# Attention and MLP in one kernel: nine of sixteen key blocks in 16-bit parts

## The chip, the cores and the metric

The kernel runs on one core of a Trainium2 chip. Its metric is the time of one execution in device microseconds (us). Engines are named as in the profile: PE is TensorE (PEld its weight loads), DVE is VectorE, ACT is ScalarE, POOL is GpSimd, SP is SyncE, which here issues most transfers.

## The reference

A token's row `x` (2048 tokens of 640 numbers, all f32) is normalised. The result feeds an attention of 32 heads of 20 numbers each, and beside it an MLP of width 1536; both are added to `x`:

```python
xn = _layernorm(x)
q, k, v = split(xn @ wqkv)                       # 32 heads of 20
scores = einsum("bhqd,bhkd->bhqk", q, k) * 20 ** -0.5
p = softmax(scores)
att = einsum("bhqk,bhkd->bhqd", p, v) @ wo
mlp = gelu(layernorm(xn) @ w1 + b1) @ w2 + b2
return x + att + mlp
```

## The kernel before

**Precision.** Most products run on pairs of 16-bit numbers: a factor is written as an upper part and a remainder, and three products of parts stand for one. The product of the probabilities with V is made in one of two ways, by key block. There are 16 blocks of 128 keys, and `SPLIT` says which way a block goes.

- *Split block* (1): the upper part of the f32 exponentials is read in place as bf16 (`upper`). The remainder is made on DVE by one subtraction of 128x1024 (`rest`, L725), into a tile `low` of f16. V is kept as two f16 parts. For each of the two heads of a pair there are three products: upper by V's first part, upper by V's second part, and low by V's first part.
- *Whole block* (0): exponentials and V stay f32, with one f32 product for each head and no work on DVE. The profile counts two rows of PE for one such product.

Before, `SPLIT` is `(1, 1, 0, 0)` four times, so eight blocks are split and eight whole.

**Front (to about 226 us).** x is normalised, turned and multiplied by wqkv; Q and K go to DRAM, V stays in `vfull`, where `vproj_out` (L408, L410) writes a block in the form that `SPLIT` asks for: for a split block one copy on ACT and one subtraction on DVE, for a whole one the copy alone. POOL writes columns of ones and zeros into V beforehand (L198, L199 for a split block, L201 for a whole one).

**Attention (about 226 to 1279 us).** A unit of work is a head pair `g`, a half of the queries `hf`, a chunk `cc` of 512 queries, and a key block `kb`. `scores` (L711) makes a block's scores for both heads of the pair on PE, and ACT takes the exponential of 128x1024 of them (L713). Units run in groups of `GRP = 4` key blocks. In each group the loop emits, in this order: scores of the first two blocks; `tick()`; `rest` of the first block; a piece of filler on PE (`other`); scores of the other two blocks; `tick()`; `rest` of the remaining blocks; and `pv(prev)`, the products of the *previous* group. The four groups of one `(g, hf, cc)` add up in one PSUM tile `pv.o` of 128x512, which ACT copies out after the last (L763).

In `pv`, `product(q, ...)` (L742) writes a quarter of 32 partitions of `pv.o`, with 32 columns of V as weights. Quarters 2a and 2a+1 belong to head a, and are added later. Products with different `q` that stand next to each other run at the same time on PE. In a group of two split and two whole blocks there are, in this order: two sets of four products on the upper parts, one set of four on low (the quarter of a head is chosen by the block's place, `2 * a + n % 2`), and one set of four f32 products, again one quarter for each block and head.

**Filler.** The MLP (`layer1` L972, `layer2` L1002) and the output projection (L1085) are cut into pieces and laid between the groups by `other`, by a credit that grows by `rate = 1.265` for each place, so how much filler stands where is fixed when the program is built. Their PSUM tile (`psM`) has one buffer, which DVE reads out (L910, L938, L1043). `tick()` issues one step of each waiting piece of DVE work: GELU (L910 to L922, with tanh on ACT at L918), the additions, and the finishing of head groups (L872 to L902).

**Buffers.** `p` (exponentials) has seven, `low` has `bufs=GRP`, that is four, and the scores' PSUM tile has three. A tile takes the buffer that came free; where its last reader is a later instruction of another engine, the writer waits for that reader.

**The end.** After the attention the projection's last pieces run alone. DVE then has reduced a check of the sums to one flag. Where it is set, `general` computes the attention again in another way, in f32 and with loops; where it is not, the program ends there.

Of the kernel before, what the change touches and what calls it, by code (L numbers as in the profile page):

```python
# [9 lines left out]
F32 = mybir.dt.float32  # L10
F16 = mybir.dt.float16
BF16 = mybir.dt.bfloat16
I32 = mybir.dt.int32
AF = mybir.ActivationFunctionType
ALU = mybir.AluOpType
AX = mybir.AxisListType
PSUM = bass.MemoryType.PSUM
DRAM = bass.MemoryType.DRAM
P = 128
S, D, H, DH, F = 2048, 640, 32, 20, 1536  # L20
KD = D // P
KF = F // P
NKB = S // P
VW = DH + 1
PAD = 32 - VW
VROW = H * VW + PAD
SPLIT = (1, 1, 0, 0) * (NKB // 4)
NPAIR = H // 2
EPS = 1e-5
TOP = 15.5  # L30
# [14 lines left out]
def mha_mlp_kernel(tc, x, wqkv, wo, w1, b1, w2, b2, out):  # L45
    nc = tc.nc
    x2 = x.rearrange("b s d -> (b s) d")
    out2 = out.rearrange("b s d -> (b s) d")

    with (  # L50
# [580 lines left out]
        with ExitStack() as scope:  # L631
# [52 lines left out]
                        yield 0.7  # L684
                split_done.append(1)

            def project(ot, acc, t0, j):
                for hf in range(2):
                    cols = slice(hf * 320, (hf + 1) * 320)
                    ps = psM.tile([P, 512], F32, tag="m", name="z")  # L690
                    n = 0
                    for k in range(KD):
                        for a, b in PASS:
                            nc.tensor.matmul(ps[:, :320], ot[:, k, a, j * P : (j + 1) * P], wov[:, k, b, cols],
                                             start=(n == 0), stop=(n == 3 * KD - 1))
                            n += 1
                    nc.vector.scalar_tensor_tensor(acc[:, cols], ps[:, :320], fo, acc[:, cols], ALU.mult, ALU.add)
                nc.sync.dma_start(out2[t0 : t0 + P, :], acc)

            nfin = 2 * len(UNITS)  # L700
            checks = list(range(nfin))
# [28 lines left out]
            def pv(units):  # L730

                g, hf, cc, kb0 = units[0][:4]
                if kb0 == 0:
                    pv.o = psO.tile([P, 512], F32, tag="o", name="o")
                    pv.begun = set()
                last = units[-1][3] == NKB - 1

                def product(q, src, v0, t):
                    nc.tensor.matmul(pv.o[32 * q : 32 * q + 32, :], src[:, v0 - PAD * (1 - q % 2) :][:, :32], t,  # L742
                                     start=q not in pv.begun, stop=last, skip_group_check=True)
                    pv.begun.add(q)

                split = [(u[3], upper(u[4]), u[5]) for u in units if SPLIT[u[3]]]
                whole = [(u[3], u[4]) for u in units if not SPLIT[u[3]]]
                of16 = lambda kb, a: 2 * PAD + kb * 2 * VROW + (2 * g + a) * 2 * VW
                of32 = lambda kb, a: PAD + kb * VROW + (2 * g + a) * VW
                for kb, up, _ in split:  # L750
                    for a in range(2):
                        product(2 * a, vhalf, of16(kb, a), up[:, a])
                        product(2 * a + 1, vhalf, of16(kb, a) + VW, up[:, a])
                for a in range(2):
                    for n, (kb, _, low) in enumerate(split):
                        product(2 * a + n % 2, vhalf, of16(kb, a), low[:, a])
                for a in range(2):
                    for n, (kb, pt) in enumerate(whole):
                        product(2 * a + n % 2, vfull, of32(kb, a), pt[:, a])
                if last:  # L760
                    if cc == 0:
                        evs[g, hf] = m1.tile([P, 2, 512], F32, tag="ev", name="ev")
                    nc.scalar.activation(evs[g, hf][:, cc], pv.o, AF.Copy)  # L763
                    if cc == 1:
                        unload(g, hf, evs.pop((g, hf)))
# [349 lines left out]
            with tc.manual_schedule():  # L1115
# [50 lines left out]
                n = 0  # L1166
# [25 lines left out]

def general(tc, nc, V, vscr, qkscr, oscr, accscr, gscale, ident, psS, psO, psM, project):

    ds = bass.ds
    nc.sync.dma_start(vscr, V)
    with (
        tc.tile_pool(name="g2", bufs=2) as g2,
        tc.tile_pool(name="g1", bufs=1) as g1,
    ):  # L1200
        with tc.For_i(0, D, DH) as r:
            qs = g1.tile([60, S], F16, name="gq")
            ks = g1.tile([60, S], F16, name="gk")
            vt = g1.tile([P, NKB, VW], F32, name="gv")
            vp = g1.tile([P, NKB, 2, DH], F16, name="gvp")
            for i, s in enumerate((0, 0, 1)):
                nc.sync.dma_start(qs[i * DH : (i + 1) * DH, :], qkscr[s, ds(r, DH), :])
            for i, s in enumerate((0, 1, 0)):
                nc.sync.dma_start(ks[i * DH : (i + 1) * DH, :], qkscr[s, ds(r + D, DH), :])
            v16 = vscr.bitcast(F16)  # L1210
            for kb in range(NKB):
                if SPLIT[kb]:
                    for i in range(2):
                        nc.sync.dma_start(vp[:, kb, i, :], v16[:, kb, ds((r // DH) * 2 * VW + i * VW, DH)])
                    nc.vector.tensor_add(vt[:, kb, :DH], vp[:, kb, 0, :], vp[:, kb, 1, :])
                else:
                    nc.sync.dma_start(vt[:, kb, :DH], vscr[:, kb, ds((r // DH) * VW, DH)])
            for qt in range(S // P):
                sf = g2.tile([P, S], F32, tag="sf", name="sf")
                m = g2.tile([P, 4], F32, tag="gm", name="gm")  # L1220
                L = g2.tile([P, 1], F32, tag="gL", name="gL")
                for i in range(2):
                    ps = psS.tile([P, 2, 512], F32, tag="s", name="gs")
                    for c in range(2):
                        kc = 2 * i + c
                        nc.tensor.matmul(ps[:, c, :], qs[:, qt * P : (qt + 1) * P],
                                         ks[:, kc * 512 : (kc + 1) * 512], start=True, stop=True)
                    nc.vector.tensor_copy(sf[:, i * 1024 : (i + 1) * 1024],
                                          ps.rearrange("p a b -> p (a b)"))
                nc.vector.tensor_reduce(m[:, 0:1], sf, AX.X, ALU.max)  # L1230
                nc.vector.tensor_scalar(sf, sf, m[:, 0:1], None, ALU.subtract)
                nc.scalar.activation(sf, sf, AF.Exp, scale=gscale, accum_out=L)
                nc.vector.reciprocal(L, L)
                nc.vector.tensor_scalar(sf, sf, L, None, ALU.mult)
                o = psO.tile([P, 512], F32, tag="o", name="go")
                for kq in range(4):
                    pt = psM.tile([P, 512], F32, tag="m", name="gt")
                    tt = g2.tile([P, 512], F32, tag="tt", name="tt")
                    for i in range(4):
                        kb = 4 * kq + i  # L1240
                        nc.tensor.transpose(pt[:, i * P : (i + 1) * P], sf[:, kb * P : (kb + 1) * P], ident)
                    nc.vector.tensor_copy(tt, pt)
                    for i in range(4):
                        kb = 4 * kq + i
                        nc.tensor.matmul(o[:DH, :P], vt[:, kb, :DH], tt[:, i * P : (i + 1) * P],
                                         start=(kb == 0), stop=(kb == NKB - 1))
                hl = g2.tile([DH, 2, P], F16, tag="ghl", name="ghl")
                nc.scalar.activation(hl[:, 0], o[:DH, :P], AF.Copy)
                nc.vector.tensor_sub(hl[:, 1], o[:DH, :P], hl[:, 0])
                nc.sync.dma_start(oscr[:, ds(r, DH), qt * P : (qt + 1) * P].rearrange("s d t -> d s t"), hl)  # L1250
    with tc.tile_pool(name="pg", bufs=2) as pg:
        for c in range(4):
            ot = pg.tile([P, KD, 2, 512], F16, tag="ot", name="ot")
            for s in range(2):
                nc.sync.dma_start(ot[:, :, s, :], oscr[s, :, c * 512 : (c + 1) * 512]
                                  .rearrange("(k p) t -> p k t", p=P))
            for j in range(4):
                acc = pg.tile([P, D], F32, tag="acc", name="acc")
                nc.sync.dma_start(acc, accscr[c * 512 + j * P : c * 512 + (j + 1) * P, :])
                project(ot, acc, c * 512 + j * P, j)  # L1260


# [25 lines left out]
```

## Time and profile before

| | |
|---|---|
| three runs | 1347.52, 1347.5, 1342.58 us, median 1347.5 |
| the profiled execution, its own time | 1344.61 us |
| its span, first to last instruction | 1342.9 us |
| granted clock of TensorE over the span | 0.999 |
| subtractions that make low (L725) | 512 of 1219 ns |
| exponentials (L713) | 1024 of 1048 ns |

The page gives each engine's busy time and its share of the span, and the chain that ended last, which is followed back from the last instruction to whatever released each step. Busy time of PE includes its modelled ends, and matmuls overlap, so the cost of a set of products is read from the distance between starts in the timeline, not from its length. Rows of the timeline give start, length, engine, line, operation, output and inputs, shape, and how many instructions were merged. Rows of stretches give a stretch, its length and the busy time of each engine in it. Rows of groups end with busy time, mean ns of one, and the idle time of the engine ahead of them with what ended it. Rows of waits give total, times and the longest.

### The profile page before, as it was taken

Reading aid. Unit: us, or ns where it says so; the run is one execution under the profiler, and the core shown is the slowest. Engines: PE = TensorE matmul, PEld = TensorE weight load, DVE = VectorE, ACT = ScalarE, POOL = GpSimd, SP = SyncE. Lnnn points to the kernel's source line nnn. Section 1 sums busy time; section 2 is a strip of 40 time slices with the busy share of each in tenths; the row PEclk is TensorE's granted clock in tenths of the full one; section 3 lists DMA queues with packets and bytes.
Section 4 is the critical chain, followed back from the end, with each engine's and each line's share of the span. In section 5 each row is a group of like instructions: output and inputs, shape, how many; then the busy total and the mean of one; then the engine's idle time right before and its main releaser. Section 6 shows DMA issues by size and latency. Waiting matters only on the chain.

```text
span 1342.9 us, 29066 instructions
## 1 busy us (share of the span) xinstructions
PE 1327.5 (99%) x11647; PEld 588.7 (44%) x11647; DVE 1056.3 (79%) x1436; ACT 1130.6 (84%) x1306; POOL 37.4 (3%) x85
## 2 busy tenths in 40 slices
PE   9999999999999999999999999999999999999997
PEld 6645546443344443434433344334334443333365
DVE  7756945998779887978897878888877988888732
ACT  7754425999999999999999999999999999999800
POOL 3010000000000000000000000000000000000000
PEclk9999999999999999999999999999999999999999
DMA  9878742111113332122322031313032323333375
GB/s 276 246 205 176 118 141 59 34 53 44 48 52 78 86 83 74 43 63 73 93 73 71 19 103 56 93 51 94 19 86 77 84 64 106 91 115 114 102 224 174
DMA packets 100153, 129.58 MB, mean 96 GB/s; under 512 B 24276, under 2 KB 66328, under 8 KB 100012
## 3 DMA queue, kind: packets, MB, share of 16 engines
q1 hardware_dynamic: 96652, 120.25, 31.8%
q0 software_dynamic: 2912, 6.90, 2.8%
q8 instruction: 93, 1.52, 0.5%
q10 hardware_dynamic: 448, 0.51, 0.1%
q14 instruction: 48, 0.39, 0.1%
HBM read 82.14 MB, written 42.51 MB: 93 GB/s over the span
## 4 chain that ended last, share of the span: by engine, by line
PE 85%; DVE 6%; DMA 4%; ACT 2%; issue 1%; SPq 1%; POOL 0%; DVEq 0%; ACTq 0%; POOLq 0%
PE o L742 28%; PE s L711 18%; PE py L1002 13%; PE pu L972 10%; PE qkp L325 7%; PE z L1085 4%; PE vp L398 3%; DVE low L725 2%; ACT p L713 1%; DMA wos<-in_A_wo_dram 1%; DMA xt<-in_A_x_dram 1%; PE warm L222 1%; DVE u L910 0%; DMA oscr<-oa 0%; DVE u L912 0%
## 5 line engine op out<-in xcount | busy, mean ns | idle before, releaser
L713 ACT ACTIVATE p<-s 128x1024 f32<-128x1024 f32 x1024 | 973.3, 1048 | 35.0 <-PE s L711 28.9
L725 DVE TENSOR_TENSOR low<-p 128x1024 f16<-128x1024 f32 x512 | 614.5, 1219 | 144.9 <-ACT p L713 144.2
L742 PE MATMUL o<-p,vfull 128*32 128x512 bf16 (+1 forms) x4096 | 430.1, 493 | 0.0
L711 PE MATMUL s<-qs,ks 61*128 61x512 f16 x2048 | 311.9, 381 | 1.1 <-ACT p L713 1.1
L711 PEld LDWEIGHTS <-ks 61*128 61x128 f16 x2048 | 61.1, 94 | 280.1 <-issue 279.0
L1002 PE MATMUL py<-w2t,hT 128*128 128x320 f16 x1152 | 178.5, 300 | 0.5 <-DVE u L910 0.3
L972 PE MATMUL pu<-xm,w1t 128*128 128x256 f16 x1440 | 178.2, 273 | 0.0
L972 PEld LDWEIGHTS <-w1t 128*128 128x128 f16 x1440 | 131.0, 98 | 64.6 <-issue 51.0
L1002 PEld LDWEIGHTS <-hT 128*128 128x128 f16 x1152 | 102.5, 98 | 88.5 <-issue 54.1
L325 PE MATMUL qkp<-xnt,wv 128*128 128x512 f16 x600 | 131.1, 379 | 2.2 <-DVE vfull L410 1.9
L742 PEld LDWEIGHTS <-vfull 128*32 128x32 f16 x3072 | 59.9, 95 | 141.0 <-issue 110.2
L742 PE MATMUL o<-low,vfull 128*32 128x512 f16 x1024 | 103.0, 378 | 2.2 <-DVE low L725 1.9
L325 PEld LDWEIGHTS <-wv 128*128 128x128 f16 x600 | 58.2, 98 | 72.2 <-DVE vfull L410 2.2
L742 PEld LDWEIGHTS o<-p,vfull 128*32 128x32 f32 x2048 | 62.7, 108 | 52.5
L1085 PE MATMUL z<-w1t,ot 128*128 128x320 f16 x480 | 67.5, 299 | 1.1 <-DVE acc L1043 1.1
L340 ACT ACTIVATE qkhl<-qkp,qks 128x1024 f16<-128x1024 f32 (+1 forms) x24 | 23.2, 967 | 53.1 <-PE qkp L325 31.7
L398 PE MATMUL vp<-wv,xnt 128*128 128x320 f16 x480 | 66.7, 299 | 0.0
L1085 PEld LDWEIGHTS <-ot 128*128 128x128 f16 x480 | 46.0, 98 | 24.1 <-issue 6.7
L398 PEld LDWEIGHTS <-xnt 128*128 128x128 f16 x480 | 46.7, 98 | 18.4
L341 DVE SCALAR_TENSOR_TENSOR qkhl<-qkp,qks,qkhl 128x1024 f16<-128x1024 f32 (+1 forms) x24 | 26.5, 1104 | 32.1 <-ACT qkhl L340 31.9
L1043 DVE SCALAR_TENSOR_TENSOR acc<-z,sc,acc 128x320 f32<-128x320 f32 x32 | 17.5, 550 | 39.7 <-PE z L1085 39.6
L763 ACT ACTIVATE ev<-o 128x512 f32<-128x512 f32 x64 | 39.4, 616 | 4.5 <-PE o L742 4.5
(188 smaller groups left out, 674.3 us busy)
## 6 DMA issues: line engine op xcount, KB each, us to landing
qkscr<-qkhl SPq DMA_DIRECT2D x40, 256.0 KB
opart<-ev SPq DMA_DIRECT2D x124, 80.0 KB
ks<-qkscr SPq DMA_DIRECT2D x120, 80.0 KB
qs<-qkscr SPq DMA_DIRECT2D x192, 40.0 KB
oa<-opart SPq DMA_DIRECT2D x32, 240.0 KB
xt<-in_A_x_dram SPq DMA_DIRECT2D x16, 320.0 KB
xscr<-xnt SPq DMA_DIRECT2D x4, 1280.0 KB
xm<-xscr SPq DMA_DIRECT2D x8, 640.0 KB
```

The lines of the kernel that those rows point to most:

```text
L325: nc.tensor.matmul(ps[:, i, :], wv[:, k, q, a, mm * P : (mm + 1) * P], xnts[c][:, k, b, :], start=(k + n == 0), stop=(k == KD - 1 and n == 2))
L340: nc.scalar.activation(hl[:, 0, i0:i1], ps[:, i0:i1], AF.Copy, scale=a)
L341: nc.vector.scalar_tensor_tensor(hl[:, 1, i0:i1], ps[:, i0:i1], a, hl[:, 0, i0:i1], ALU.mult, ALU.subtract)
L398: nc.tensor.matmul(ps[:, hf, :320], xnts[c][:, k, a, j * P : (j + 1) * P], wv[:, k, 2, b, hf * 320 : (hf + 1) * 320], start=(n == 0), stop ...
L711: nc.tensor.matmul(ps[:, a, :], ks[64 * a : 64 * a + 61, kb * P : (kb + 1) * P], qs[64 * a : 64 * a + 61, cc * 512 : (cc + 1) * 512], star ...
L713: nc.scalar.activation(pt, ps, AF.Exp, scale=QS)
L725: nc.vector.tensor_sub(low, pt, upper(pt))
L742: nc.tensor.matmul(pv.o[32 * q : 32 * q + 32, :], src[:, v0 - PAD * (1 - q % 2) :][:, :32], t, start=q not in pv.begun, stop=last, skip_gr ...
L763: nc.scalar.activation(evs[g, hf][:, cc], pv.o, AF.Copy)
L972: nc.tensor.matmul(ps[:, i], w1v[:, k, (f + i) // 4, a, fo_ : fo_ + P], xnt[:, k, b, :], start=(n == 0), stop=(n == 3 * KD - 1))
L1002: nc.tensor.matmul(ps[:, :320], hTs[mc][:, f, a, j * P : (j + 1) * P], w2v[:, f, b, hf * 320 : (hf + 1) * 320], start=(n == 0), stop=(n == ...
L1085: nc.tensor.matmul(ps[:, :320], ot[:, k, a, j * P : (j + 1) * P], wov[:, k, b, h * 320 : (h + 1) * 320], start=(n == 0), stop=(n == 3 * KD ...
```

## The change

Block 6 becomes split, so nine blocks are split and seven are whole. Every second group of a `(g, hf, cc)` (blocks 4 to 7) then holds three split blocks and one whole. Where a set would be left with one block for both quarters of a head, its 512 tokens are halved: tokens 0 to 255 go to the head's even quarter and 256 to 511 to its odd one. That happens to the third low part and to the lone f32 block of this group. The general path is written as two nested loops (tokens outside, heads inside) that make one token tile of one head at a time, with fewer transfers and with the pattern of `SPLIT` built into its slices; `project` now takes rows instead of an offset.

```diff
-SPLIT = (1, 1, 0, 0) * (NKB // 4)
+SPLIT = (1, 1, 0, 0, 1, 1, 1, 0) + (1, 1, 0, 0) * 2
...
-                def product(q, src, v0, t):
-                    nc.tensor.matmul(pv.o[32 * q : 32 * q + 32, :], src[:, v0 - PAD * (1 - q % 2) :][:, :32], t,
-                                     start=q not in pv.begun, stop=last, skip_group_check=True)
+                def product(q, src, v0, t, c0=0, c1=512):
+                    nc.tensor.matmul(pv.o[32 * q : 32 * q + 32, c0:c1], src[:, v0 - PAD * (1 - q % 2) :][:, :32],
+                                     t[:, c0:c1], start=q not in pv.begun, stop=last, skip_group_check=True)
                     pv.begun.add(q)
+
+                def whole_tokens(a, n, alone, src, v0, t):
+
+                    if alone:
+                        product(2 * a, src, v0, t, 0, 256)
+                        product(2 * a + 1, src, v0, t, 256, 512)
+                    else:
+                        product(2 * a + n % 2, src, v0, t)
...
-                for a in range(2):
-                    for n, (kb, _, low) in enumerate(split):
-                        product(2 * a + n % 2, vhalf, of16(kb, a), low[:, a])
+                for n0 in range(0, len(split), 2):
+                    for a in range(2):
+                        for n, (kb, _, low) in enumerate(split[n0 : n0 + 2]):
+                            whole_tokens(a, n, n0 + 1 == len(split), vhalf, of16(kb, a), low[:, a])
                 for a in range(2):
                     for n, (kb, pt) in enumerate(whole):
-                        product(2 * a + n % 2, vfull, of32(kb, a), pt[:, a])
+                        whole_tokens(a, n, len(whole) == 1, vfull, of32(kb, a), pt[:, a])
...
 def general(tc, nc, V, vscr, qkscr, oscr, accscr, gscale, ident, psS, psO, psM, project):
...
+        tc.For_i(0, S, P) as t,
     ):
         with tc.For_i(0, D, DH) as r:
```

More of the change, by code (lines that the diff above doesn't have):

```diff
@@ L685, in prep_late, with project @@
                 split_done.append(1)
-            def project(ot, acc, t0, j):
+            def project(ot, acc, rows):
                 for hf in range(2):
@@ L693, in project @@
                         for a, b in PASS:
-                            nc.tensor.matmul(ps[:, :320], ot[:, k, a, j * P : (j + 1) * P], wov[:, k, b, cols],
+                            nc.tensor.matmul(ps[:, :320], ot[:, k, a, :], wov[:, k, b, cols],
                                              start=(n == 0), stop=(n == 3 * KD - 1))
@@ L697, in project @@
                     nc.vector.scalar_tensor_tensor(acc[:, cols], ps[:, :320], fo, acc[:, cols], ALU.mult, ALU.add)
-                nc.sync.dma_start(out2[t0 : t0 + P, :], acc)
+                nc.sync.dma_start(out2[rows, :], acc)
             nfin = 2 * len(UNITS)
@@ L1196, in general @@
     nc.sync.dma_start(vscr, V)
+    assert SPLIT == tuple(int(i % 4 < 2 or i == 6) for i in range(NKB))
     with (
         tc.tile_pool(name="g2", bufs=2) as g2,
-        tc.tile_pool(name="g1", bufs=1) as g1,
+        tc.For_i(0, S, P) as t,
     ):
         with tc.For_i(0, D, DH) as r:
[L1202 to L1260, printed above, removed]
+            qs = g2.tile([60, P], F16, name="gq")
@@ new lines, in general @@
+            ks = g2.tile([60, S], F16, name="gk")
+            vr = g2.tile([P, NKB, VW], F32, name="gv")
+            vt = g2.tile([P, NKB, DH], F32, name="gvt")
+            nc.sync.dma_start(qs[: 2 * DH], qkscr[:, ds(r, DH), ds(t, P)])
+            nc.sync.dma_start(qs[2 * DH :], qkscr[0, ds(r, DH), ds(t, P)])
+            nc.sync.dma_start(ks[:DH], qkscr[0, ds(r + D, DH), :])
+            nc.sync.dma_start(ks[DH:], qkscr[:, ds(r + D, DH), :])
+            nc.sync.dma_start(vr, vscr[:, :, ds((r // DH) * VW, VW)])
@@ new lines, in general @@
+            vp = vr.bitcast(F16)
+            for b in (slice(0, None, 4), slice(1, None, 4), slice(6, 7)):
+                nc.vector.tensor_add(vt[:, b, :], vp[:, b, :DH], vp[:, b, VW : VW + DH])
+            sf = g2.tile([P, S], F32, tag="sf", name="sf")
+            m = g2.tile([P, 4], F32, tag="gm", name="gm")
+            L = g2.tile([P, 1], F32, tag="gL", name="gL")
+            for i in range(2):
+                ps = psS.tile([P, 2, 512], F32, tag="s", name="gs")
+                for c in range(2):
+                    kc = 2 * i + c
+                    nc.tensor.matmul(ps[:, c, :], qs, ks[:, kc * 512 : (kc + 1) * 512], start=True, stop=True)
+                nc.vector.tensor_copy(sf[:, i * 1024 : (i + 1) * 1024],
+                                      ps.rearrange("p a b -> p (a b)"))
@@ new lines, in general @@
+            nc.vector.tensor_reduce(m[:, 0:1], sf, AX.X, ALU.max)
+            nc.vector.tensor_scalar(sf, sf, m[:, 0:1], None, ALU.subtract)
+            nc.scalar.activation(sf, sf, AF.Exp, scale=gscale, accum_out=L)
+            nc.vector.reciprocal(L, L)
+            nc.vector.tensor_scalar(sf, sf, L, None, ALU.mult)
+            o = psO.tile([P, 512], F32, tag="o", name="go")
+            for kq in range(4):
+                pt = psM.tile([P, 512], F32, tag="m", name="gt")
+                tt = g2.tile([P, 512], F32, tag="tt", name="tt")
+                kb0 = 4 * kq
+                for i in range(4):
+                    nc.tensor.transpose(pt[:, i * P : (i + 1) * P], sf[:, (kb0 + i) * P :][:, :P], ident)
+                nc.vector.tensor_copy(tt, pt)
+                for i in range(4):
+                    nc.tensor.matmul(o[:DH, :P], (vt if SPLIT[kb0 + i] else vr)[:, kb0 + i, :DH], tt[:, i * P : (i + 1) * P],
+                                     start=(kb0 + i == 0), stop=(kb0 + i == NKB - 1))
@@ new lines, in general @@
+            hl = g2.tile([DH, 2, P], F16, tag="ghl", name="ghl")
+            nc.scalar.activation(hl[:, 0], o[:DH, :P], AF.Copy)
+            nc.vector.tensor_sub(hl[:, 1], o[:DH, :P], hl[:, 0])
+            nc.sync.dma_start(oscr[:, ds(r, DH), ds(t, P)].rearrange("s d t -> d s t"), hl)
+        ot = g2.tile([P, KD, 2, P], F16, tag="ot", name="ot")
+        for s in range(2):
+            nc.sync.dma_start(ot[:, :, s, :], oscr[s, :, ds(t, P)].rearrange("(k p) t -> p k t", p=P))
+        acc = g2.tile([P, D], F32, tag="acc", name="acc")
@@ L1264 @@
+        nc.sync.dma_start(acc, accscr[ds(t, P), :])
+        project(ot, acc, ds(t, P))
 _INS = ["A_x", "A_wqkv", "A_wo", "B_w1", "B_b1", "B_w2", "B_b2"]
```

## The prediction

> A *sweep* below is one head pair's 512 query tokens against all 16 key blocks: 64 of them, each of four groups of four key blocks. Only the second group (blocks 4 to 7) of each sweep changes its work.
>
> **What bounds the kernel now.** I read the page first (engines, the chain that ended last), then busy time by stretch, then the order of time inside one group.
>
> ```profile
> span 1342.9 us, 29066 instructions
> ...
> PE 1327.5 (99%) x11647; PEld 588.7 (44%) x11647; DVE 1056.3 (79%) x1436; ACT 1130.6 (84%) x1306; POOL 37.4 (3%) x85
> ...
> PE 85%; DVE 6%; DMA 4%; ACT 2%; issue 1%; SPq 1%; POOL 0%; DVEq 0%; ACTq 0%; POOLq 0%
> ```
>
> PE carries 85% of the chain, so TensorE's order of work sets most of the time. But DVE holds 6% of it, some 80 us: there are places where TensorE runs at VectorE's pace. The stretches show how near the others are.
>
> ```profile
> 0.00:226.32 226.32, 222.75 (x1421) 127.70 (x1422) 143.90 (x333) 118.83 (x176) 22.44 (x67) 1.00 0.71 181
> 226.32:1279.31 1052.99, 1048.17 (x9801) 419.99 (x9800) 891.75 (x1064) 1011.76 (x1131) 15.01 (x18) 1.00 0.26 72
> ```
>
> Columns: stretch, length, then busy time of PE, weight loads, DVE, ACT, POOL, then granted clock. In the attention (second row) the clock is 1.00, ACT is busy 96% of 1053 us and DVE 85%. ACT has 41 us left, DVE 161 us. Neither average is full; the question is where these idle times lie. I cut the attention at each sweep's first product: in 17 sweeps DVE has less than 1.13 us idle (the price of one more subtraction, below), in the other 47 more. Those 17 alone:
>
> ```profile
> 226.32:243.38 17.06, 17.06 (x162) 7.27 (x161) 16.71 (x22) 16.38 (x20) 0.00 (x0) 1.00 0.00 1
> ...
> 260.25:276.56 16.31, 15.96 (x154) 6.54 (x153) 16.10 (x20) 16.15 (x20) 0.00 (x0) 1.00 0.24 70
> ...
> 1198.58:1215.06 16.48, 16.48 (x154) 6.19 (x152) 15.39 (x27) 15.45 (x17) 0.85 (x1) 1.00 0.24 64
> sum 281.13, PE 279.35 PEld 112.57 DVE 272.31 ACT 273.78 POOL 1.76; mean PE 16.43 PEld 6.62 DVE 16.02 ACT 16.10 POOL 0.10
> ```
>
> They have 281.13 - 272.31 = 8.8 us of DVE idle in all. The row at 260.25 has 0.21 us, which I take for what merely lies between instructions, so about 0.2 x 17 = 3.4 us of it can take no work and 5.4 us can. The 17 sweeps lie in twelve places: 226 to 277 (three sweeps), 293, 408 to 442 (two), 508, 541, 672, 804, 838, 919 to 952 (two), 1050 to 1083 (two), 1116, 1199.
>
> **The change on TensorE.** One group of today, and its neighbours:
>
> ```profile
> 704.55 1.22 DVE L725 TENSOR_TENSOR low<-p 128x1024 f16<-128x1024 f32 x1 [0.96 <-ACT p L713]
> 705.68 0.35 PEld L742 LDWEIGHTS <-vfull 128*32 128x32 f16 x12 [0.42 <-issue]
> 705.68 0.64 PE L742 MATMUL o<-p,vfull 128*32 128x512 bf16 x8
> ...
> 706.15 0.39 PE L742 MATMUL o<-low,vfull 128*32 128x512 f16 x4
> ...
> 706.30 1.22 DVE L725 TENSOR_TENSOR low<-p 128x1024 f16<-128x1024 f32 x1
> 706.36 1.04 PE L742 MATMUL o<-p,vfull 128*32 128x512 f32 x8
> 707.33 0.11 PEld L711 LDWEIGHTS <-ks 61*128 61x128 f16 x4 [0.84 <-issue]
> ...
> 710.61 0.39 PE L742 MATMUL o<-low,vfull 128*32 128x512 f16 x4
> ```
>
> Four products, one in each 32-column quarter of the array, run side by side; I call them a quartet. Starts give the price: two bf16 quartets take 706.15 - 705.68 = 0.47 us, 0.235 each; the quartet on low takes 0.21; the f32 work of two whole blocks takes 0.97 up to the next scores. It is one quartet in two passes, whose second pass a cut at 1068.3 shows by itself:
>
> ```profile
> 1067.38 1.03 PE L742 MATMUL o<-p,vfull 128*32 128x512 f32 x8
> ...
> 1067.81 0.60 PE L742 MATMUL o<-p,vfull 128*32 128x512 f32 x4
> 1068.34 0.61 PE L711 MATMUL s<-qs,ks 61*128 61x512 f16 x4
> ```
>
> A pass is 0.43 us, and 0.10 of the last 0.53 is the turn to the scores. Block 6 changes sides, so group 2 of a sweep gets a third bf16 quartet (+0.235; by the later starts +0.21 at least) and a half-length quartet on its low part, and the lone whole block 7 has both its f32 passes halved. Short quartets exist in the trace at 128 columns:
>
> ```profile
> 162.06 0.52 PE L370 MATMUL norms<-sq,heads 128*32 128x128 bf16 x24
> 162.51 3.70 PE L398 MATMUL vp<-wv,xnt 128*128 128x320 f16 x26
> ```
>
> Six of them take 0.45 us with both turns, at most 0.075 each. So time follows columns there, and issue of the loads does not hold it; 256 columns lie between 0.105 (half of 0.21) and, say, 0.13. I take 0.105. The halved passes save 0.43; if a half pass cost a bf16 quartet plus some start, they would save 0.33. Sum for a sweep: 0.235 + 0.105 - 0.43 = -0.09 us, bounds -0.115 and +0.035. Over 64 sweeps: **-5.8 us**, bounds -7.4 and +2.2. The operand order of f32 and 16-bit products within an accumulation stays, so no further turn is added.
>
> The loads are hidden too: by the load row above, the 12 loads of three quartets have ended 0.35 us after 705.68, while two quartets of matmuls fill 0.47. A rule of the Trainium skill ("TensorE: Matmul & The Clock Gate", Part 3, The mechanism) says otherwise: a weight load overlaps with running matmuls only when its row group differs, and here all four quarters use all 128 rows. By that rule the trace disagrees; if it held for the added quartets, it would make the third rival below.
>
> **The change on VectorE.** Each sweep gets a ninth subtraction (L725).
>
> ```profile
> L725 DVE TENSOR_TENSOR low<-p 128x1024 f16<-128x1024 f32 x512 | 614.5, 1219 | 144.9 <-ACT p L713 144.2
> ```
>
> It shows 1.22 us; two in a row take 2.35 us (at 1059.68, below), so one more costs 2.35 - 1.22 = 1.13 us. That is 64 x 1.13 = 72 us more on DVE. It is issued right behind block 5's, in the second half of the group. Where is it hidden? In the row at 706.30 the subtraction ends at 707.52 and TensorE asks for it at 710.61: 3.1 us of lead. The 144.2 us that DVE waits for exponentials take it up soon after. In such a sweep it costs nothing. Where the cover is gone looks like this:
>
> ```profile
> 1059.12 0.49 PE L742 MATMUL o<-low,vfull 128*32 128x512 f16 x4
> ...
> 1059.68 2.35 DVE L725 TENSOR_TENSOR low<-p 128x1024 f16<-128x1024 f32 x2
> ...
> 1070.35 1.22 DVE L725 TENSOR_TENSOR low<-p 128x1024 f16<-128x1024 f32 x1
> 1070.74 0.64 PE L742 MATMUL o<-p,vfull 128*32 128x512 bf16 x8
> 1071.21 0.81 PE L742 MATMUL o<-low,vfull 128*32 128x512 f16 x4
> ...
> 1071.63 1.25 PE L742 MATMUL o<-p,vfull 128*32 128x512 f32 x8
> ```
>
> The quartet at 1071.21 needs the part that DVE ends at 1071.57; the f32 work starts 0.42 after it, not 0.21. There DVE has no idle, lead is zero, and 1.13 us more is 1.13 us on TensorE. In the 17 sweeps 17 x 1.13 = 19.2 us come in, 5.4 us find room, **13.8 us** do not. Not all of that must show: at the end of each of the twelve places lateness up to the next lead is forgiven as DVE idle returns. I choose 0.4 us for each place, between no lead (the row at 1071.21) and the whole 1.13: 4.8 us. Cost **+9.0 us**; bounds 0 (leads cover everything) and 16 (nothing is forgiven and some of the 47 sweeps with a short lead stall too). Behind DVE also stand the reads that free the single psM buffer of the filler (L910, L938) and the input of tanh (L916), so lateness reaches TensorE by three ways, not one.
>
> In the 17 sweeps a shorter TensorE wins nothing, as DVE sets the pace: of the 5.8 us I count 47/64, **-4.2 us**.
>
> **An added wait.** There are four buffers for low. Groups of two need exactly four in flight; a group of three makes it five, so twice a sweep (block 6's own, and block 9's) a subtraction waits until TensorE has read an older part, in the products that are issued later. Behind it in DVE's order stand the filler's GELU and sums. Block 6's part starts after block 5's, 1.13 us later than DVE's earliest, when the quartet on low has usually been read (above, 1059.12 + 0.49 = 1059.61, DVE at 1059.68). Block 9's can wait some 0.5 us, in sweeps where DVE runs early and so has idle. I cost it at nothing; if the cover is gone it is some 0.1 us for each of the 128, mostly in idle sweeps, which the upper bound of 16 holds.
>
> **ACT and the rest.** ACT's instructions stay.
>
> ```profile
> ACT p L713 <- PE s L711: 28.9, 122, 0.5
> PE s L711 <- ACT p L713: 1.1, 4, 0.3
> ```
>
> TensorE waits 1.1 us for ACT, ACT 28.9 us for TensorE; 5.8 us saved fit into the latter. In the front block 6 of V gets one more subtraction and a memset in place of another:
>
> ```profile
> L410 DVE SCALAR_TENSOR_TENSOR vfull<-vp,vfull x8: 808/820/828, 55.4 to 213.1; 128x640 f16<-128x640 f32 x8
> L199 POOL MEMSET vfull<- x8: 324/448/552, 1.6 to 3.8; 128x32 f16 x8
> ```
>
> 0.82 us on DVE near 170 us; DVE is 143.90 of 226.32 us busy in this stage (the first row of the stretches), so it may hide. Between 0 and 0.8, I take +0.4. The memset (0.45 us) is done near 4 us, far ahead of V: nothing. The general path stands behind a flag; if it were taken, the trace would show its lines, and it ends with the projection instead. Ahead of it every queue, SP's and POOL's included, issues the same transfers in the same order: nothing.
>
> **Sum.** -4.2 + 9.0 + 0.4 = +5.2 us. The profiled execution took 1344.6 us (span 1342.9 and 1.7 around it): 1349.8. The three runs, 1342.58 to 1347.52, have their median 2.9 above it; I add about half of that, 1.5: **1351.3 us**.
>
> **Rivals.** They use two rows more, of the waits and of the loads:
>
> ```profile
> PE o L742 <- DVE low L725: 1.9, 1, 1.9
> ```
>
> ```profile
> L742 PEld LDWEIGHTS <-vfull 128*32 128x32 f16 x3072 | 59.9, 95 | 141.0 <-issue 110.2
> ```
>
> 1. *The leads cover DVE.* TensorE saves 5.8 us everywhere and DVE's 72 us go into its 161 us of idle: 1344.6 - 5.8 + 0.4, about 1339 to 1342. For it: PE's direct waits for low are 1.9 us in the whole table of waits. Against it: the 6% of DVE in the chain and the twelve full places.
> 2. *DVE becomes the bound in full.* Nothing is forgiven, the reads of psM stall as well and the buffer wait bites: +16 - 4.2 + 0.4, about 1357 and up to 1362. It decides from the point where a place's lead is under 1.13 us. For it: 0.21 us idle in whole sweeps.
> 3. *Weight loads show.* The loads of the two added quartets, 0.095 us each, do not hide: -0.09 turns into +0.10 a sweep, +6.4 us, with DVE's 9.0 about 1361. The load row at 705.68 speaks against it.
> 4. *No effect on TensorE*, since halved passes cost as much as whole ones: excluded but for the bound above.
>
> **How the numbers follow.** Forecast 0.55 (1346 to 1357), rival 1 0.20, rival 2 0.20, rival 3 0.03, others 0.02. Some 0.5% is what a measurement can tell from no change: 6.7 us, so 1340.8 and 1354.2 are the marks. Of the forecast 0.36 lies under 1354.2 and 0.19 above; of rival 1, 0.05 lies under 1340.8. Slower 0.19 + 0.20 + 0.03 = 0.42; faster 0.05; the rest 0.53. Range: 1340 to 1361, the cases of both signs; the forecast's own is 1346 to 1357.
>
> **What would show it.** Right: in the second group three bf16 quartets and a short one on low, f32 passes of 0.21 us; 576 subtractions; PE's products some 6 us less by pitch; DVE's share of the chain clearly above 6%, with new stretched quartets on low or late filler starts at 226 to 310, 408 to 442 and 1050 to 1083. Wrong: a chain with DVE at 6% or less and a span under 1340 (rival 1), a quartet pitch over 0.3 us (rival 3), or TensorE waiting in sweeps where DVE had idle (the buffer wait).

## The result, and the profile after

| | before | after |
|---|---|---|
| six runs each, median | 1343.9 us (1342.58 to 1347.52) | 1355.65 us (1352.43 to 1361.24) |
| ratio, 95% interval | | 1.0074 (1.0055 to 1.0092) |
| profiled execution, its own time | 1344.61 us | 1352.58 us |
| its span | 1342.9 us | 1350.6 us |

The kernel became slower by 0.74%, some 10 us by the ratio (the two medians lie 11.8 apart). The forecast was +5.2 us on the profiled execution, which came out 8.0 us longer. First the page after the change: engines, and the chain by engine and by line.

```profile
PE 1328.9 (98%) x12159; PEld 602.4 (45%) x12159; DVE 1126.1 (83%) x1501; ACT 1132.6 (84%) x1306; POOL 37.7 (3%) x86
...
PE 73%; DVE 16%; issue 4%; ACT 3%; DMA 3%; SPq 2%; DVEq 0%; ACTq 0%
PE o L742 22%; PE s L711 14%; PE py L1011 11%; PE qkp L325 10%; DVE low L725 9%; PE pu L981 7%; PE vp L398 5%; PE z L1094 5%; ACT p L713 2%; DVE u L919 1%; DVE u L921 1%; DVE u L929 1%; DVE w L925 1%; DVE hT L930 1%; DVE hT L931 1%
```

DVE's busy time grew by 69.8 us, about the 72 that were counted, and its share of the chain from 6% to 16%: TensorE now runs at VectorE's pace in many more places. One changed group in a place where DVE is early (timeline of TensorE, start and length first):

```profile
715.14 0.86 PE L742 MATMUL o<-p,vfull 128*32 128x512 bf16 x12
715.83 0.50 PE L742 MATMUL o<-low,vfull 128*32 128x512 f16 x8
716.15 0.61 PE L742 MATMUL o<-p,vfull 128*32 128x256 f32 x8
716.69 0.60 PE L711 MATMUL s<-qs,ks 61*128 61x512 f16 x4
```

Three bf16 quartets take 0.69 us (0.47 for two before), the quartet and a half on low 0.32 (0.21 before), the halved f32 work 0.54 up to the scores (0.97 before). Sum 1.55 against 1.65: 0.10 less, where 0.09 was forecast. And one in a place where DVE is full:

```profile
430.24 2.36 DVE L725 TENSOR_TENSOR low<-p 128x1024 f16<-128x1024 f32 x2
430.73 0.86 PE L742 MATMUL o<-p,vfull 128*32 128x512 bf16 x12
431.42 0.48 PE L742 MATMUL o<-low,vfull 128*32 128x512 f16 x4
...
432.64 0.29 PE L742 MATMUL o<-low,vfull 128*32 128x256 f16 x4 [0.74 <-DVE low L725]
432.75 0.62 PE L742 MATMUL o<-p,vfull 128*32 128x256 f32 x8
...
433.73 1.94 ACT L713 ACTIVATE p<-s 128x1024 f32<-128x1024 f32 x2 [1.11 <-PE s L711]
433.98 0.69 DVE L919 TENSOR_TENSOR u<-pu,r2f 128x512 f32<-128x512 f32 x1
...
434.72 0.57 PE L1011 MATMUL py<-w2t,hT 128*128 128x320 f16 x3 [0.81 <-DVE u L919]
```

The second subtraction of the first row is block 6's; it ends at 432.60, and the half quartet that needs it starts at 432.64 after 0.74 us of standing still. Two microseconds later the filler waits 0.81 us for the read of its PSUM buffer, which stands behind the same subtractions and one of the next group on DVE. ACT loses 1.11 us in between.

Now the same cut as in the prediction. In stretches the columns are length, then busy time of PE, weight loads, DVE, ACT, POOL, then granted clock. First the whole attention, then the sum over the same 17 sweeps, each from its first product to the next sweep's:

```profile
224.53:1288.54 1064.01, 1049.56 (x10313) 433.58 (x10312) 960.88 (x1128) 1013.95 (x1131) 15.02 (x18) 1.00 0.26 72
```

```profile
sum 291.09, PE 283.03 PEld 115.74 DVE 287.59 ACT 276.90 POOL 2.40; mean PE 16.65 PEld 6.81 DVE 16.92 ACT 16.29 POOL 0.14
```

The 17 sweeps went from 281.13 to 291.09 us, **+10.0**. DVE is idle in 3.5 us of them, the 0.2 us a sweep that merely lie between instructions. The other 47 went from 1052.99 - 281.13 = 771.86 to 1064.01 - 291.09 = 772.92 us, **+1.1**, where -4.2 was forecast. The front (226.32 to 224.53) and the end (63.59 to 62.03) came out 1.8 and 1.6 us shorter, which makes 7.7 for the span.

One sweep has to be read with care. Sweep 62 (counted from 0, in order of time) has a length of its own in every profile. Here it is in four kernels, in this order: without block 6's subtraction, with it in the 17 full sweeps alone, changed, and changed with the general path of before (the other three are experiments below).

```profile
1239.35:1256.98 17.63, 15.74 (x153) 5.71 (x152) 12.19 (x15) 15.89 (x19) 0.00 (x0) 1.00 0.47 151
```

```profile
1250.01:1269.22 19.21, 17.27 (x152) 5.83 (x150) 13.30 (x16) 16.07 (x19) 0.00 (x0) 0.91 0.43 138
```

```profile
1255.99:1274.29 18.30, 15.74 (x152) 5.72 (x151) 13.23 (x16) 15.89 (x19) 0.00 (x0) 1.00 0.46 145
```

```profile
1255.52:1274.95 19.43, 17.26 (x153) 5.82 (x151) 14.36 (x17) 15.99 (x19) 0.00 (x0) 0.91 0.42 136
```

The last two have the same attention and differ by 1.1 us. DVE waits there for a transfer, in the second of the four for 4.25 us, and TensorE waits for the low part behind it:

```profile
1262.57 0.69 DVE L911 TENSOR_TENSOR oa<-oa 80x512 f32<-80x512 f32 x1 [4.25 <-DMA oa<-opart]
...
1264.45 0.40 PE L748 MATMUL o<-low,vfull 128*32 128x512 f16 x3 [1.94 <-DVE low L729]
```

In two of the four the granted clock over the sweep is 0.91 besides. Two kernels below that differ in a buffer alone differ by 1.8 us here (17.73 and 19.56). So a difference of 1 to 2 us in this sweep says nothing of the subtraction; the lengths of the sweeps 3 and 28, read below, repeat within 0.02 us between kernels with the same work in them.

### The profile page after: what moved, and what is told of

It reads as the page before. It is cut to its first block, busy times and chain, and to the rows that moved or that the text cites. A ratio compares the mean times of both kernels' runs of the same rounds, so it can differ in the third digit from the quotient of the medians.

```text
span 1350.6 us, 30257 instructions
## 1 busy us (share of the span) xinstructions
PE 1328.9 (98%) x12159; PEld 602.4 (45%) x12159; DVE 1126.1 (83%) x1501; ACT 1132.6 (84%) x1306; POOL 37.7 (3%) x86
## 4 chain that ended last, share of the span: by engine, by line
PE 73%; DVE 16%; issue 4%; ACT 3%; DMA 3%; SPq 2%; DVEq 0%; ACTq 0%
PE o L742 22%; PE s L711 14%; PE py L1011 11%; PE qkp L325 10%; DVE low L725 9%; PE pu L981 7%; PE vp L398 5%; PE z L1094 5%; ACT p L713 2%; DVE u L919 1%; DVE u L921 1%; DVE u L929 1%; DVE w L925 1%; DVE hT L930 1%; DVE hT L931 1%
## 5 line engine op out<-in xcount | busy, mean ns | idle before, releaser
L725 DVE TENSOR_TENSOR low<-p 128x1024 f16<-128x1024 f32 x576 | 685.4, 1218 | 89.3 <-ACT p L713 84.1
L742 PE MATMUL o<-p,vfull 128*32 128x512 bf16 (+2 forms) x4352 | 420.6, 462 | 0.0
L742 PEld LDWEIGHTS <-vfull 128*32 128x32 f16 x3584 | 76.1, 95 | 173.1 <-issue 127.2
L742 PE MATMUL o<-low,vfull 128*32 128x512 f16 (+1 forms) x1280 | 117.4, 357 | 7.0 <-DVE low L725 5.6
```

Source lines behind the costliest of these rows:

```text
L725: nc.vector.tensor_sub(low, pt, upper(pt))
L742: nc.tensor.matmul(pv.o[32 * q : 32 * q + 32, c0:c1], src[:, v0 - PAD * (1 - q % 2) :][:, :32], t[:, c0:c1], start=q not in pv.begun, stop ...
```

## The experiments

The theory: TensorE saves some 6 us (64 times the forecast's 0.09 to the 0.10 of the rows above; the expectations take 0.097, that is 6.2), and the ninth subtraction takes back more, mostly in the 17 full sweeps. Rivals: the rewritten end of the program, the changed products themselves, and the waits for a buffer of low. Ratios are to the kernel of before, run beside each.

**The end of the program.** The changed kernel with `general` and `project` as before.

> The changed kernel with the general path of before. Theory (VectorE's ninth subtraction takes the time): as the changed kernel, ratio to before 1.005 to 1.009. Rival (the rewritten end of the program costs or saves something): back towards 1.000, or above 1.010.

Measured: 1.0081 (1.0057 to 1.0106). The rewritten path, which does not run here, has no part in it that could be told from noise.

**TensorE's part alone.**

```diff
 if SPLIT[kb]:
+    if kb == 6:
+        unit.append(latest[0])
+        return
     low = ptp.tile([P, 2, 512], F16, tag="low", name="low", bufs=GRP)
     nc.vector.tensor_sub(low, pt, upper(pt))
+    latest[:] = [low]
...
+latest = []
```

> The changed kernel without block 6's subtraction: its products read block 5's low part, so TensorE has the changed work and VectorE the old one. It leaves out block 6's remainder. Theory: TensorE's saving alone, by the distances between starts 64 x 0.097 = 6.2 us, less where VectorE sets the pace: ratio 0.995 to 0.997. Rival (the changed products themselves cost time, by loads or turns): 1.000 or above.

Measured: 0.9937 (0.9914 to 0.9959), some 8 us faster, more than the theory's range gives, though the interval reaches down to 5.5 us. The attention and the 17 sweeps of this kernel:

```profile
224.18:1271.25 1047.07, 1042.71 (x10313) 432.79 (x10312) 891.72 (x1064) 1010.29 (x1131) 15.01 (x18) 1.00 0.26 73
```

```profile
sum 279.87, PE 278.08 PEld 115.81 DVE 272.09 ACT 273.63 POOL 1.76; mean PE 16.36 PEld 6.81 DVE 16.01 ACT 16.10 POOL 0.10
```

The attention is 5.9 us shorter than before, nearly the 6.2: 1.3 in the 17 sweeps and 771.86 - 767.20 = 4.7 in the 47 (0.5 of it in sweep 62). So the saving of the products is real, loads and all, and the loss lies wholly in what block 6's subtraction brings.

**VectorE's part alone.** The kernel of before, with one more subtraction a sweep whose result nobody reads. A tile of ones moves into the front's pool to make room for it.

```diff
+elif kb == 6:
+    more = m1.tile([P, 2, 512], F16, tag="more", name="more")
+    nc.vector.tensor_sub(more, pt, upper(pt))
```

> The kernel of before with block 6's subtraction added on VectorE, its result unused, in a tile of its own, so that no buffer of low is missing and TensorE's work stays. Theory: all of the loss and none of the saving, 12 to 16 us, ratio 1.009 to 1.012. Rival (the loss is the wait for a buffer of low, which this kernel does not have): 1.000 to 1.003.

Measured: 1.0100 (1.0072 to 1.0129), within the forecast. Its attention:

```profile
225.75:1292.28 1066.53, 1054.02 (x9801) 420.95 (x9800) 959.60 (x1128) 1014.65 (x1131) 15.01 (x18) 1.00 0.26 71
```

That is 13.5 us longer than before. This kernel has no half quartet that waits and no missing buffer, and loses all the same: time on DVE is the cause, not the new dependence.

**Where it is lost.** Block 6's subtraction in some sweeps only; in the others the products read block 5's part, as above. The edit is against that kernel and leaves block 6 out in the 17 full sweeps; the second kernel has `not in`.

```diff
+FULL = {0, 1, 2, 4, 11, 12, 17, 19, 27, 35, 37, 42, 43, 50, 51, 54, 59}
...
-    if kb == 6:
+    if kb == 6 and 2 * ORDER.index((unit[0], unit[1])) + unit[2] in FULL:
```

> The changed kernel with block 6's subtraction only in the 47 sweeps where VectorE had over 1.13 us idle; in the other 17 the products read block 5's low part, so block 6's remainder is left out there. Theory (the loss sits in the 17 full sweeps): most of TensorE's saving, 0.994 to 0.998. Rival (the loss goes with the number of subtractions, 47 of 64): 1.002 to 1.004.

> The opposite: block 6's subtraction only in the 17 full sweeps, its remainder left out in the other 47. Theory: nearly the whole loss, 1.002 to 1.007. Rival (by number, 17 of 64): 0.996 to 0.998.

Measured: 0.9971 (0.9958 to 0.9985) with the 47, and 1.0034 (1.0018 to 1.0050) with the 17. The second lies above what its number would give, the first below, so most of the loss sits with the full sweeps. The profile of the first, attention and then the 17:

```profile
223.99:1274.46 1050.47, 1044.34 (x10313) 433.23 (x10312) 942.96 (x1111) 1010.69 (x1131) 15.01 (x18) 1.00 0.26 73
```

```profile
sum 279.83, PE 278.01 PEld 115.81 DVE 272.08 ACT 273.61 POOL 2.41; mean PE 16.35 PEld 6.81 DVE 16.00 ACT 16.09 POOL 0.14
```

and of the second:

```profile
223.61:1283.47 1059.86, 1049.17 (x10313) 432.84 (x10312) 909.41 (x1081) 1013.59 (x1131) 15.02 (x18) 1.00 0.26 72
```

```profile
sum 291.06, PE 282.99 PEld 115.70 DVE 287.57 ACT 277.15 POOL 1.76; mean PE 16.65 PEld 6.81 DVE 16.92 ACT 16.30 POOL 0.10
```

Against the kernel without the subtraction (279.87 and 767.20 us): the 17 subtractions cost 291.06 - 279.87 = 11.2 us in their own sweeps. The other 47 sweeps of that kernel are 768.80 - 767.20 = 1.6 us longer, but that is sweep 62 alone (17.63 and 19.21 us above), so no cost behind the full sweeps is shown. The 47 subtractions cost 770.64 - 767.20 = 3.4 us in theirs. The changed kernel's attention is 1064.01 - 1047.07 = 16.9 us longer: 11.2 in the 17 sweeps and 772.92 - 767.20 = 5.7 in the 47, of which 0.7 is sweep 62. One subtraction costs 11.2 / 17 = 0.66 us in a full sweep. In the others the mean, 0.07, hides that most cost nothing: five of the 47 make up 2.8 of the 3.4 us. The longest of them is sweep 28, first without its subtraction and then with it:

```profile
684.13:701.21 17.08, 17.05 (x165) 6.99 (x164) 15.49 (x18) 16.31 (x19) 0.00 (x0) 1.00 0.32 89
```

```profile
684.45:702.56 18.11, 17.60 (x166) 6.92 (x164) 16.62 (x19) 16.30 (x19) 0.00 (x0) 1.00 0.28 84
```

DVE has 17.08 - 15.49 = 1.59 us idle there, more than the subtraction's 1.13, and yet the sweep grows by 1.03. The timeline shows why, again without and then with it:

```profile
690.52 4.63 DVE L728 TENSOR_TENSOR low<-p 128x1024 f16<-128x1024 f32 x4
...
693.03 0.39 PE L747 MATMUL o<-low,vfull 128*32 128x512 f16 x4
...
695.70 1.23 DVE L728 TENSOR_TENSOR low<-p 128x1024 f16<-128x1024 f32 x1 [0.55 <-ACT p L713]
```

```profile
691.97 4.63 DVE L729 TENSOR_TENSOR low<-p 128x1024 f16<-128x1024 f32 x4
...
694.37 0.40 PE L748 MATMUL o<-low,vfull 128*32 128x512 f16 x3 [0.42 <-DVE low L729]
```

Without it the first two of the four subtractions end near 692.83 (half of 4.63 behind 690.52) and their products start at 693.03: 0.2 us of lead. The idle time that follows, 0.55 us at 695.70, comes too late to help them. Sweep 3, right behind the first three full ones, shows what happens to lateness that is put off: it takes 16.82 us where only the full sweeps have the subtraction, 16.83 where only the others have it, and 17.74 in the changed kernel, where both do:

```profile
276.73:294.47 17.74, 16.88 (x173) 7.87 (x171) 17.36 (x23) 16.57 (x20) 0.00 (x0) 1.00 0.18 51
```

**The buffers of low.** Five instead of four, so that none of the 128 subtractions waits for TensorE. Room for the fifth comes from a tile of ones that moved into the front's pool.

```diff
-    low = ptp.tile([P, 2, 512], F16, tag="low", name="low", bufs=GRP)
+    low = ptp.tile([P, 2, 512], F16, tag="low", name="low", bufs=GRP + 1)
```

> The changed kernel with five buffers for low, so that none of the 128 subtractions waits for TensorE. Theory: the waits lie where VectorE has idle, so as the changed kernel within 1.5 us, ratio 1.005 to 1.009. Rival (the waits set the loss): 0.996 to 1.000.

> The changed kernel with five buffers for low once more, to narrow its interval. If the buffers cost nothing, its ratio goes towards the changed kernel's 1.0074; if they cost 2 to 3 us, it stays near 1.0053.

> The kernel with block 6's subtraction in the 47 sweeps alone (its remainder left out in the other 17), and five buffers for low, so that no subtraction waits for TensorE. It asks what the 47 sweeps' own loss is made of. Theory: half of it or more is short leads and not the buffers, so within 2 us of the same kernel with four, ratio 0.995 to 0.998. Rival (the buffers): 0.992 to 0.994, as without any subtraction.

Measured: 1.0053 (1.0035 to 1.0071), again 1.0045 (1.0027 to 1.0063), and with the 47 sweeps alone 0.9971 (0.9958 to 0.9984), the same as with four. The attention and the 17 sweeps of the first:

```profile
223.89:1289.43 1065.54, 1051.35 (x10313) 433.74 (x10312) 959.39 (x1128) 1013.96 (x1131) 15.01 (x18) 1.00 0.26 71
```

```profile
sum 291.11, PE 283.05 PEld 115.88 DVE 287.62 ACT 276.88 POOL 2.53; mean PE 16.65 PEld 6.82 DVE 16.92 ACT 16.29 POOL 0.15
```

With four buffers the table of waits lists these, and with five none:

```profile
DVE low L725 <- PE o L742: 4.1, 5, 1.3
```

The attention is not shorter than with four buffers (1065.54 and 1064.01 us; 1.2 of the difference is sweep 62), nor are the 17 sweeps (291.11 and 291.09). The waits for a buffer cost nothing there. The two ratios are 3 to 5 us under those of the changed kernel with either general path, with intervals that overlap. By what was expected of the second run, a ratio that stays near 1.0053 speaks for 2 to 3 us that the buffers cost; the profiles show no such cost in the attention. If the difference is more than chance, it lies outside the attention, and this stays open.

**Another engine.** Block 6's subtraction on POOL, which is 3% busy.

```diff
-    nc.vector.tensor_sub(low, pt, upper(pt))
+    (nc.gpsimd if kb == 6 else nc.vector).tensor_sub(low, pt, upper(pt))
```

> The changed kernel with block 6's subtraction on POOL. Theory: VectorE is as before and TensorE saves 6.2 us, so 0.993 to 0.998, if POOL needs under 3 us for one and is not held up by its own transfers. Rival (POOL is too slow, stands behind its 16 transfers for xb, or slows VectorE down): 1.000 or above, with TensorE waiting for POOL.

Measured: 1.0605 (1.0584 to 1.0626), the rival, and for at least two reasons at once. Groups by shape, then the table of waits:

```profile
L725 DVE TENSOR_TENSOR low<-p 128x1024 f16<-128x1024 f32 x512 | 646.5, 1283 | 157.1 <-ACT p L713 154.0 <-PE o L742 2.5
L725 POOL TENSOR_TENSOR low<-p 128x1024 f16<-128x1024 f32 x64 | 159.9, 2499 | 740.4 <-ACT p L713 527.8 <-DVE low L725 58.6 <-DVE hT L931 32.0
```

```profile
PE o L742 <- POOL low L725: 43.0, 10, 11.0
```

POOL needs 2.5 us, and TensorE's stops for it are up to 11 us long. Part of that is its queue. Around 355 us:

```profile
354.63 0.88 POOL L1001 DMA_DIRECT2D xb<-in_B_b_dram  x1 [19.69 <-DVE low L725]
355.26 2.18 POOL L725 TENSOR_TENSOR low<-p 128x1024 f16<-128x1024 f32 x1
357.50 0.29 PE L742 MATMUL o<-low,vfull 128*32 128x256 f16 x4 [4.43 <-POOL low L725]
```

The subtraction stands behind a transfer that POOL issues, and TensorE waits 4.43 us. And VectorE is no better off. Its busy time on this kernel, from the page, and then on the kernel without block 6's subtraction; both have 512 on DVE:

```profile
PE 1354.0 (95%) x12159; PEld 608.6 (43%) x12159; DVE 1129.4 (79%) x1437; ACT 1136.3 (80%) x1306; POOL 196.0 (14%) x150
```

```profile
PE 1323.4 (99%) x12159; PEld 602.8 (45%) x12159; DVE 1056.5 (79%) x1437; ACT 1128.7 (84%) x1306; POOL 37.7 (3%) x86
```

At 298 us both engines are at a subtraction at the same time (two rows of the timeline):

```profile
298.93 2.92 DVE L725 TENSOR_TENSOR low<-p 128x1024 f16<-128x1024 f32 x1
```

```profile
297.96 2.81 POOL L725 TENSOR_TENSOR low<-p 128x1024 f16<-128x1024 f32 x1 [15.66 <-DVE w L925]
```

DVE's subtraction takes 2.92 us instead of 1.22: it ends at 301.85, 1.08 us after POOL's (300.77), as if it had begun when POOL's ended. So with POOL's 64 beside them the same 1437 instructions of DVE take 73 us more, all that was to be taken off it. The Trainium skill ("SBUF — State Buffer", Terms) says that the two engines share a pair of ports to SBUF as an exclusive lock, so that the loser blocks; this trace agrees. The granted clock over this run's attention was lower too, 0.98 where it was 1.00 without the subtraction; what share of the loss that has was not tested.

**Ten and seven blocks.** These have the general path of before. Ten: `SPLIT = (1, 1, 0, 0, 1, 1, 1, 0) * 2`.

> Ten split blocks: the last group but one of a sweep (blocks 12 to 15) is cut like the second too. TensorE saves another 6.2 us, VectorE gets another 72 us where some 90 us of waiting are left. Theory: the loss grows faster than in proportion, 1.018 to 1.035. Rival (each added block costs what the first did): 1.013 to 1.017.

Measured: 1.0279 (1.0260 to 1.0298). The second added block costs 2.0%, the first 0.74%. DVE's wait for exponentials, the idle time that more work could fill, shrank:

```profile
DVE low L725 <- ACT p L713: 39.2, 64, 4.2
PE o L742 <- DVE low L725: 19.0, 29, 2.2
```

The first was 144.2 us before, and the second, TensorE's wait, 1.9. Seven: `SPLIT = (1, 1, 0, 0, 1, 0, 0, 0) + (1, 1, 0, 0) * 2`.

> Seven split blocks: the second group of a sweep has one split and three whole, so VectorE loses a subtraction a sweep (72 us less) and TensorE gains 0.097 us (6.2 us in all). The kernel of before has some 8 us of TensorE standing still at places where VectorE is late, and that is all there is to win. Theory: 0.998 to 1.003, far from the mirror image of nine. Rival (in proportion, the mirror of nine): 0.992 to 0.995.

Measured: 1.0243 (1.0223 to 1.0263), which neither side had expected. TensorE shows why:

```profile
705.37 0.28 PE L742 MATMUL o<-low,vfull 128*32 128x256 f16 x4
705.48 1.91 PE L742 MATMUL o<-p,vfull 128*32 128x512 f32 x12
707.32 0.61 PE L711 MATMUL s<-qs,ks 61*128 61x512 f16 x4
```

The changed kernel halves a block only where it is the only whole one. With three, a head's third product goes to the quarter that its first one holds, and must stand in line: 1.84 us, where 1.5 quartets by the prices above would take about 1.4. Over 64 groups the f32 work alone adds 64 x (1.84 - 0.97) = 56 us, and the bf16 quartet and half quartet on low that fall away take back some 0.34 us each, 22: 34 us, where 2.43% is 33. So it says nothing of VectorE, but prices the halving. With the three taken in pairs and the last halved (against the kernel just measured):

```diff
-for a in range(2):
-    for n, (kb, pt) in enumerate(whole):
-        whole_tokens(a, n, len(whole) == 1, vfull, of32(kb, a), pt[:, a])
+for n0 in range(0, len(whole), 2):
+    for a in range(2):
+        for n, (kb, pt) in enumerate(whole[n0 : n0 + 2]):
+            whole_tokens(a, n, n0 + 1 == len(whole), vfull, of32(kb, a), pt[:, a])
```

> Seven split blocks again, with the three whole blocks of the second group taken in pairs of which the last is halved over a head's two quarters, as the changed kernel does with low. TensorE then has the mirror of the change, 64 x 0.097 = 6.2 us more, VectorE 72 us less. Theory (only the places where TensorE stands still for VectorE can be won back, 3 to 6 us): 1.000 to 1.003. Rival (the mirror of nine): 0.992 to 0.995.

Measured: 1.0017 (0.9999 to 1.0036), 2.3 us. The same f32 work now takes 1.40 us instead of 1.84:

```profile
709.84 1.46 PE L742 MATMUL o<-p,vfull 128*32 128x512 f32 x16
711.24 0.61 PE L711 MATMUL s<-qs,ks 61*128 61x512 f16 x4
```

The attention, 1052.99 us before:

```profile
224.66:1282.82 1058.16, 1053.78 (x10057) 427.84 (x10056) 824.23 (x1000) 1011.84 (x1131) 15.00 (x18) 1.00 0.26 72
```

TensorE pays its 6.2 us, and VectorE's relief of 67 us there (891.75 to 824.23) wins 1 us of it back by the attention, 4 by the ratio. Seven, eight, nine and ten split blocks stand at 1.0017, 1, 1.0074 and 1.0279. Seven can't be told from eight by its interval, nine and ten are worse; no version tried that keeps the whole computation beats the kernel of before.

## Why the prediction was right, and where a size was off

The time lay in the range and on the side that the forecast gave, a little slower. By the prediction's own mark of 0.5% the kernel is clearly slower, a case to which it gave 0.42; it gave 0.53 to no change that could be told. Part of the nearness is luck: by cause, both large terms were too small, and the errors have opposite signs. The saving was 5.9 us in the attention instead of the 4.2 that were counted, and the subtraction cost 16.9 instead of 9.0, a little above the bound of 16. In the attention that is +11.0, where +4.8 was forecast; a front and an end 3.4 us shorter brought the profile nearer to the forecast. Point by point:

- *TensorE, -5.8 us.* Right: 5.9 us in the attention of the kernel without the subtraction, 0.10 us a group by starts. The rival in which weight loads show is out, and with it the Trainium skill's rule beside it ("TensorE: Matmul & The Clock Gate", Part 3, The mechanism), for this layout: three quartets with their twelve loads take 0.69 us.
- *DVE in the 17 full sweeps, +9.0 us.* Right in place and nearly in size: +10.0, which is 11.2 of cost less 1.3 of saving, though the prediction held that a shorter TensorE wins nothing there. Its parts hold less well. In the kernel with the 17 alone DVE is busy 909.41 - 891.72 = 17.7 us longer in the attention, not 19.2, so a subtraction adds 1.04 us and not 1.13. Of these, 287.57 - 272.09 = 15.5 fall into the 17 sweeps and 2.2 are put off into the sweeps behind, where 4.8 were assumed to be forgiven.
- *The saving counted only in the other 47 sweeps, -4.2 us.* This is the term that was mis-sized: it came out at +1.1. The saving itself was there (4.7), but the prediction let a subtraction cost nothing wherever a sweep had more than 1.13 us idle. In the runs the 47 sweeps lost 5.7 us: 3.4 by their own subtractions, 0.9 in sweep 3, where lateness of the full sweeps meets one more subtraction, 0.7 in sweep 62, which moves by itself, and some 0.7 in small pieces. Idle time in a sweep is not enough: in sweep 28 it came behind the products that needed the low parts (that the smaller losses have this cause too is likely, not shown). The prediction's upper bound named this ("some of the 47 sweeps with a short lead stall too"); its middle left it out. Lateness put off was forgiven where the sweep behind had no subtraction of its own, and not always where it had.
- *The buffer wait at nothing.* Right in the attention.
- *The front, +0.4 us, and the rest at nothing.* Nothing that single profiles can tell: the front lies between 223.6 and 227.3 us in these kernels.
- *The 1.5 us added for the median.* Unfounded, and of the right sign by luck: with six runs the median of before is 1343.9, under its profiled execution, while that of the changed kernel is 3 us above its own.

Rival 1 (leads cover DVE) is refuted by the subtraction alone, 1.0100. The 1.9 us of waiting for low that spoke for it is, in the kernel before, the stall of sweep 62 behind a transfer. Rival 2 (DVE in full) named a sum, 1357, that is nearer to the median of 1355.65 than the forecast's 1351.3, and its price for DVE, 16 us, is close to the 16.9 measured. Its mechanism holds in part: the reads of psM do stall (0.81 us above) and short leads cost time in the 47 sweeps, but its buffer wait costs nothing, and in the full sweeps 11.2 us were lost, not 13.8. What decided was the second half of the upper bound, the short leads.

## What to carry to other kernels

Before work is moved from a full engine to one that is 80% busy, cut the idle time of the second by the period of the pipeline, and count only what lies ahead of the next consumer in each period; here 161 us of idle could not take 72 us of work for less than 17. Two kernels test the cause: one with the products and no added work, one with the added work in chosen periods. Before a difference of a microsecond between two profiles is explained, look for the periods that differ between profiles of the same work; here one of 64 moved by 1 to 2 us. A helper that is idle need not bring relief: POOL, 3% busy, slowed VectorE by as much as it took over.

## What was not expected

POOL's subtraction of 2.5 us took as much from VectorE (73 us over 64) as VectorE's own would have. And the way from seven over eight and nine to ten split blocks is steep on one side only: one subtraction a sweep less on VectorE won back 1 to 4 of TensorE's 6.2 us, while one more cost 17 us of attention.
